# Attention over packed keys followed by a squared-relu MLP: batch 0 in two pieces with float keys, scores on 16 tiles from batch 3, small stages of both quads merged

## The chip, the cores and the metric

The kernel runs on one core of one Trainium2 chip. The metric is device time in microseconds (us), the median of the runs shown. The core has five engines that run their own instruction streams in order and wait for each other by semaphores: TensorE (PE, matmuls; its weight loads are listed as PEld), VectorE (DVE), ScalarE (ACT), GpSimd (POOL) and SyncE (SP). Transfers are issued from SP, ACT or POOL and run on 16 shared DMA engines.

## The reference

Eight batches of eight heads, 576 positions, head dimension 64, and 32 "pack" queries per head.

```python
def sm_attn(qq, kk, vv):
    s = scale * np.matmul(qq, kk.transpose(0, 1, 3, 2))
    s = s - np.max(s, axis=-1, keepdims=True)
    a = np.exp(s)
    a = a / (np.sum(a, axis=-1, keepdims=True) + 1e-09)
    return np.matmul(a, vv)
p_packed = sm_attn(p, k, v)             # 32 x 64 per head
out = sm_attn(q, p_packed, p_packed)    # 576 x 64 per head
...
x = np.ascontiguousarray(attn_out.transpose(0, 2, 1, 3)).reshape(B * S, H * D)   # 4608 x 512
h = x @ w_in                            # 512 x 2048
r = np.maximum(h, 0.0)
return ((r * r) @ w_out).astype(np.float32)                                       # 2048 x 512
```

All inputs are float32 with small random values; the output is float32.

## The kernel before

**One list sets the order of everything.** The string `ORDER` (L41 to L123) holds one word per step. `run` (L573) executes the words one after another in a manual schedule, so that each engine gets its instructions in the order of the words, and so does each DMA queue. There is no other scheduler. A letter after a colon names the engine of the step: `v` DVE, `a` ACT, `p` POOL.

**Tiles.** Four heads make a quad, so a batch has quads 0 and 1. A 128-partition tile of a quad holds four heads of 32 rows each.

The steps of a quad `bq` (batch b, quad q), in the order in which they depend on each other:

- `Lk`, `Lq`, `Lv`: loads of k, q, v, issued on POOL's queue, which turns float32 into bfloat16 in flight (`load1`, L229).
- `kT`, `qT`: DVE transposes of 32x32 blocks (L279, L285).
- `s1`: scores of the pack queries against the keys (`scores`, L295), 32x32 matmuls over 288 columns. One quad uses 4 of the array's 16 tiles of 32x32; where both quads are given in one step (`s12`, three characters) and the batch is in `PAIRED` (2 to 7), the second quad's heads are swapped by `group`, so that both quads use different tiles, 8 at a time. Such a step goes through four rounds: two halves of 288 columns by two halves of the 64-deep contraction.
- `m1` maximum (DVE, L316), `x1` exponential (ACT, L321), `rd` reciprocal of its sum (DVE, L328).
- `eT` six PE transposes of the exponentials (L339), `eo` their copy out of PSUM, `pv` 24 matmuls with v (L352), `pp` the normalised packed rows (L360, L362), `bd` a DVE transpose of them (L367), `pt` a PE transpose of them (L372) and `po` its copy out.
- `s2`: scores of the 576 positions against the 32 packed rows, the same form as `s1`.
- `t2` DVE transpose out of PSUM (L383), `m2` maximum over the 32 (L387), `sb` subtraction, called `d` (L391, DVE or POOL), `x2` exponential (L396, ACT), `su` sums and reciprocals (L401, L403), `a2` normalised weights, called `a` (L407, DVE or POOL), `aT` DVE transpose into `a2T` (L415).
- `w0`, `w1`: the packed rows times `w_in`, 8 matmuls each for 2 x 512 columns (L422), and `W0`, `W1`, their copies out of PSUM to `wp`.

The weights of the second attention are thus folded into the MLP: instead of forming x, the kernel multiplies `wp` (packed rows times w_in) with `a2T`.

The steps of the MLP:

- `h`: layer 1 for one block of 128 of the 2048 hidden columns (L438). From batch 1 on a step is `hb.half.block`, two matmuls of 288 positions. In batch 0 a step `h0.block` covers both halves in a two-bank PSUM tile, four matmuls.
- `r`: relu out of PSUM (ACT L444 or DVE L446), `q`: the square into `gT` (DVE L479).
- `o`: layer 2 (L490). `o<tile>.<j>` is two matmuls of 512 columns; 8 such steps make a tile of 128 positions, 36 tiles in all. Tiles 0 to 3 take the quarters of `w_out` in the order 0, 2, 1, 3.
- `c`: the copy of a finished tile out of PSUM, and its two stores, issued on SP (L510). The last tile is split over ACT and DVE.

`Wi`, `Wo` load `w_in` and `w_out` in quarters on POOL's queue; `P0`, `P1`, `Pr`, `Pt` bring and transpose the pack queries (`p_f` is loaded as float32 on SP at the start); `Z<n>` puts n matmuls of zeros on PE (L263), 95 in all, 32 of them before the first scores.

**PSUM.** `psa` has two tiles of two banks, for scores, transposes, `pv` and `w`. The other four banks change their use: three `spare` and one `idle` for batch 0's attention, then two two-bank tiles `pair` for batch 0's layer 1, then two `pso` and two `early` for tiles 0 to 3, and two `psh` for layer 1 later.

Of the kernel before, what the change touches and what calls it, by code (L numbers as in the profile page):

```python
# [31 lines left out]
PAIRED = range(2, 8)  # L32
# [9 lines left out]
Lk00 Lk01 Lq00 kT00 P0 Z32 s100 kT01 I m100 x100 Z5 s101 m101 x101 Lq01 P1 Z7 eT00 Lv00 eo00:a Lk10 Z10 pv00 rd00  # L42
qT00 rd01 qT01 pp00:v bd00 eT01 kT10 Lv01 Z3 s200 Wi00 Wi01 pt00 eo01:a Lk11 Z5 pv01 s110 pp01:a t200 pt01 Wi10 bd01
m200 sb00:p m110 s201 x110 t201 x200 m201 su00 Z10 eT10 po01:v eo10:a a200:v Z12 w001 sb01:p po00:a x201 su01 Wi11
aT00 w000 Lv11 a201:p kT11 W001:a Z11 s111 Lv10 W000:a aT01 h0.8 m111 h0.11 r0.8:a h0.9 r0.11:v h0.2 x111 r0.9:a
w101 q0.8 h0.3 r0.2:v W101:a Lq11 eT11 eo11:a rd11 h0.10 Lq10 q0.9 rd10 w100 r0.3:v W100:a h0.1 r0.10:v h0.0 q0.3
pv11 Wo0 r0.1:a q0.11 Pr r0.0:v h0.5 q0.2 pp11:a h0.6 pv10 r0.5:a qT11 r0.6:a pt11 bd11 q0.1 h0.14 pp10:a q0.10
r0.14:a h0.12 s211 h0.15 q0.0 r0.12:a h0.7 r0.15:a po11:v qT10 r0.7:a w011 Wo2 t211 Lk21 h0.13 q0.6 W011:a q0.5 h0.4
bd10 r0.4:a w111 s210 r0.13:v Wo1 o0.0 q0.7 m211 sb11:v o2.0 x211 W111:a t210 o2.1 Lk20 m210 o3.0 Wo3 o1.0 o0.1 o0.2
q0.15 o1.1 su11 o1.2 Pt pt10 po10:a q0.4 o2.2 o3.1 w010 Lv20 w110 o0.3 Lq21 o3.2 o3.3 o0.4 q0.13 o2.3 W010:a Lv21  # L50
o1.3 kT21 q0.12 W110:a kT20 a211:p o1.4 q0.14 sb10:p x210 su10 o1.5 o0.5 s12 o2.4 o2.5 a210:p m120 x120 o0.6 m121
o1.6 aT11 aT10 o0.7 c0:v o1.7 x121 o2.6 c1:a o2.7 h1.0.0 qT21 h1.0.6 eT20 eT21 rd21 r1.0.6:v rd20 r1.0.0:a o3.4
h1.0.4 Lq20 eo20:a h1.0.2 pv20 eo21:v pv21 r1.0.2:v r1.0.4:a h1.0.1 pp20:v h1.0.5 pt20 pp21:v c2:a r1.0.1:a r1.0.5:a
o3.5 po20:a bd21 h1.0.12 h1.0.3 w020 q1.0.2 o3.6 r1.0.12:a r1.0.3:a h1.0.7 h1.0.13 q1.0.0 Lk30 qT20 o3.7 W020:a bd20
o4.0 r1.0.13:a c3:a r1.0.7:v q1.0.1 h1.0.10 q1.0.6 h1.0.11 q1.0.3 s22 r1.0.10:a h1.0.8 r1.0.11:a r1.0.8:a h1.0.9
Lq30 o4.1 t220 h1.0.14 r1.0.9:a o4.2 t221 q1.0.4 r1.0.14:a h1.1.0 r1.1.0:a pt21 h1.0.15 m221 o4.3 po21:a h1.1.2
r1.0.15:a w021 w120 q1.0.5 h1.1.10 o5.0 sb21:v r1.1.2:a W021:a o4.4 h1.1.8 m220 x221 Lv31 r1.1.10:a sb20:v o5.1 Lk31
r1.1.8:a x220 o4.5 h1.1.3 r1.1.3:a h1.1.11 o4.6 r1.1.11:a kT30 W120:a h1.1.4 kT31 r1.1.4:a w121 q1.0.7 h1.1.1 o5.2
o4.7 r1.1.1:a h1.1.6 o5.3 su20 W121:a su21 Lq40 h1.1.5 r1.1.5:a r1.1.6:v c4:a o5.4 s13 a221:v h1.1.7 q1.1.0 r1.1.7:a
h1.1.14 q1.1.5 o5.5 r1.1.14:a h1.1.15 r1.1.15:a a220:v Lk40 o5.6 aT21 o5.7 q1.1.1 q1.1.2 h1.1.12 q1.1.3 Lk41 aT20  # L60
c5:a h1.1.13 Lq31 r1.1.12:a o6.0 o6.1 h1.1.9 r1.1.13:a r1.1.9:a o6.2 Lv41 m131 h2.0.2 q1.1.4 r2.0.2:a h2.0.3 o6.3
m130 h2.0.0 r2.0.3:a o6.4 h2.0.4 kT40 q1.1.7 r2.0.0:a x130 o7.0 h2.0.8 r2.0.4:a o6.5 Lv30 r2.0.8:a eT30 x131 h2.0.6
rd30 o7.1 eo30:v h2.0.7 o7.2 eT31 r2.0.6:a q1.1.6 o6.6 o6.7 qT30 r2.0.7:a rd31 qT31 q2.0.1 h2.0.1 h2.0.14 pv30
eo31:a r2.0.1:a pv31 o7.3 pp31:a c6:a r2.0.14:v h2.0.5 q2.0.0 o7.4 h2.0.10 pp30:a r2.0.5:v o7.5 bd30 r2.0.10:a
h2.0.12 pt30 r2.0.12:a o7.6 h2.0.9 h2.0.11 po30:a kT41 w030 bd31 w130 r2.0.11:a W030:a r2.0.9:v q2.0.3 h2.1.6 q2.0.2
r2.1.6:a h2.0.13 o7.7 r2.0.13:a o8.0 W130:v c7:a h2.0.15 h2.1.7 r2.0.15:a s23 q2.0.4 h2.1.0 r2.1.7:v q2.0.7 o8.1
r2.1.0:a h2.1.14 t230 o8.2 t231 h2.1.12 r2.1.14:a Lq41 q2.0.6 m231 o8.3 o8.4 Lv40 r2.1.12:a pt31 q2.0.5 h2.1.1 o8.5
o9.0 h2.1.15 r2.1.1:a h2.1.4 r2.1.4:a o8.6 r2.1.15:a o9.1 o8.7 m230 h2.1.10 po31:v sb31:v o9.2 h2.1.13 x231 o9.3
o9.4 r2.1.10:a sb30:v su31 r2.1.13:a h2.1.8 q2.1.3 c8:a w131 w031 q2.1.0 h2.1.11 o9.5 x230 r2.1.8:v r2.1.11:a a231:v
W031:a q2.1.6 h2.1.2 o9.6 r2.1.2:v h2.1.5 su30 o9.7 a230:v q2.1.7 h2.1.3 aT31 W131:a r2.1.5:a o10.0 o10.1 o10.2 s14  # L70
h2.1.9 aT30 c9:a r2.1.3:a o10.3 q2.1.1 h3.0.8 o10.4 o10.5 r2.1.9:a r3.0.8:a h3.0.2 h3.0.0 m140 q2.1.4 x140 m141
r3.0.2:a x141 q2.1.2 q2.1.5 o11.0 eT40 eo40:v h3.0.6 o11.1 r3.0.0:a rd41 o11.2 h3.0.3 eT41 r3.0.6:a h3.0.1 qT40 qT41
r3.0.3:a o10.6 Lk50 eo41:a r3.0.1:v h3.0.7 o10.7 rd40 q3.0.1 pv40 pv41 r3.0.7:a pp40:v q3.0.0 h3.0.4 h3.0.5 pt40
o11.3 r3.0.4:a h3.0.9 c10:v Lk51 o11.4 r3.0.5:v r3.0.9:a q3.0.4 o11.5 h3.0.10 o11.6 po40:a pp41:a h3.0.12 pt41 bd40
r3.0.10:a q3.0.3 h3.0.14 r3.0.14:v r3.0.12:a o11.7 h3.0.15 bd41 w140 po41:a q3.0.2 w040 r3.0.15:v h3.1.2 W040:a
o12.0 W140:a o12.1 r3.1.2:v h3.0.11 o12.2 o12.3 kT51 q3.0.7 r3.0.11:v h3.1.0 kT50 s24 h3.1.4 r3.1.0:v c11:a o12.4
t241 o12.5 r3.1.4:a o12.6 h3.1.5 o12.7 r3.1.5:a h3.0.13 q3.0.5 r3.0.13:a o13.0 h3.1.6 o13.1 m241 c12:a sb41:v h3.1.3
# [48 lines left out]
class Kernel:  # L126
# [138 lines left out]
    def bank32(self, b, name):  # L265

        if b == 0:
            return self.banks("spare").tile([P, 512], F32, name=name, tag="s")
# [359 lines left out]
```

## Time and profile before

| | |
|---|---|
| runs: median (lowest to highest) | 251.08 us (250.28 to 251.39), 3 runs |
| span of the profiled execution | 248.6 us |
| PE busy | 237.1 us, 2415 matmuls |
| DVE busy | 194.2 us, 411 instructions |
| ACT busy | 145.7 us, 316 |
| POOL busy | 45.8 us, 75 |
| layer 2 (L490), busy | 144.2 us |
| layer 1 (L438), busy | 91.9 us |
| read from HBM, written | 37.22 MB, 9.44 MB |

The span reaches from the first to the last instruction; the time of a run is longer by what lies around it. Matmuls are pipelined, so the busy time of one line overlaps that of the next: a mean duration in the groups (379 ns for L490) is a latency, and the distance from one matmul to the next is read from the chain of waits, where matmuls of one kind follow each other. The groups of the profile give line, engine, operation, output and inputs with their shapes, count, then busy time and mean duration in ns of one, then idle time of the engine before them and what ended it.

### The profile page before, as it was taken

Reading aid. Unit: us, or ns where it says so; the run is one execution under the profiler, and the core shown is the slowest. Engines: PE = TensorE matmul, PEld = TensorE weight load, DVE = VectorE, ACT = ScalarE, POOL = GpSimd, SP = SyncE. Lnnn points to the kernel's source line nnn. Section 1 sums busy time; section 2 is a strip of 40 time slices with the busy share of each in tenths; the row PEclk is TensorE's granted clock in tenths of the full one; section 3 lists DMA queues with packets and bytes.
Section 4 is the critical chain, followed back from the end, with each engine's and each line's share of the span. In section 5 each row is a group of like instructions: output and inputs, shape, how many; then the busy total and the mean of one; then the engine's idle time right before and its main releaser. Section 6 shows DMA issues by size and latency. Waiting matters only on the chain.

```text
span 248.6 us, 6041 instructions
## 1 busy us (share of the span) xinstructions
PE 237.1 (95%) x2415; PEld 132.2 (53%) x2447; DVE 194.2 (78%) x411; ACT 145.7 (59%) x316; POOL 45.8 (18%) x75
## 2 busy tenths in 40 slices
PE   8998899998999999999999999999999999999992
PEld 5655554465556554655456555655555555555540
DVE  1888899978988899979887998898897798644710
ACT  2346784476968748755764658676957555353100
POOL 8329634350401500033000230010000000000000
PEclk9999999999999999999999999999999999999997
DMA  6999999999791992269812794252121213211323
GB/s 112 203 207 205 206 197 209 197 142 259 161 171 64 157 211 45 46 93 187 185 42 45 135 130 122 64 90 56 42 45 42 45 42 82 49 42 44 70 63 82
DMA packets 23358, 28.52 MB, mean 115 GB/s; under 512 B 4257, under 2 KB 14753, under 8 KB 23329
## 3 DMA queue, kind: packets, MB, share of 16 engines
q0 software_dynamic: 16880, 18.55, 47.1%
q1 hardware_dynamic: 6288, 9.44, 15.0%
q8 instruction: 19, 0.31, 0.5%
q10 hardware_dynamic: 160, 0.13, 0.2%
q14 instruction: 11, 0.08, 0.1%
HBM read 37.22 MB, written 9.44 MB: 188 GB/s over the span
## 4 chain that ended last, share of the span: by engine, by line
PE 81%; DMA 10%; issue 2%; DVE 2%; POOL 2%; ACT 1%; SPq 0%; ACTq 0%; POOLq 0%
PE ps_o L490 48%; PE ps_h L438 24%; DMA v_b<-in_v_dram 4%; PE ps_wp L422 3%; PE ps_s L295 3%; DMA w_in_bf<-in_moe_w_in_dram 3%; DMA out_dram<-o_sb 3%; PE ps_e1T L339 1%; PE ps_pv L352 1%; POOL k_b L242 1%; DVE mx L387 1%; POOL d L391 0%; ACT r L444 0%; POOL q_b L242 0%; PE ps_ppT L372 0%
## 5 line engine op out<-in xcount | busy, mean ns | idle before, releaser
L490 PE MATMUL ps_o<-w_out_bf,gT 128*128 128x512 bf16 x544 | 144.2, 379 | 2.0 <-issue 0.5
L444 ACT ACTIVATE r<-ps_h 128x288 bf16<-128x288 f32 (+1 forms) x181 | 73.1, 426 | 55.9 <-PE ps_h L438 47.5
L438 PE MATMUL ps_h<-a2T,wp 128*128 128x288 bf16 x512 | 91.9, 286 | 1.4 <-ACT r L444 1.4
L490 PEld LDWEIGHTS <-gT 128*128 128x128 bf16 x576 | 54.9, 98 | 42.1 <-issue 3.3
L438 PEld LDWEIGHTS <-wp 128*128 128x128 bf16 x512 | 47.4, 98 | 44.4 <-issue 7.7
L479 DVE TENSOR_TENSOR gT<-r 128x576 bf16<-128x576 bf16 x128 | 54.7, 448 | 5.2 <-ACT r L444 4.9
L446 DVE TENSOR_SCALAR r<-ps_h 128x288 bf16<-128x288 f32 (+1 forms) x59 | 28.5, 484 | 20.0 <-PE ps_h L438 18.8
L332 ACT CAST wp<-ps_wp 128x1024 bf16<-128x1024 f32 x29 | 28.9, 1016 | 3.8 <-PE ps_wp L422 3.7
L332 ACT COPY o_sb<-ps_o 128x512 f32<-128x512 f32 x27 | 15.9, 588 | 10.8 <-PE ps_o L490 9.4
L321 ACT ACTIVATE e<-ps_s,nm 128x576 bf16<-128x576 f32 x16 | 11.8, 736 | 13.0 <-DVE nm L316 13.0
L233 POOL DMA_DIRECT2D v_b<-in_v_dram x16 | 11.1, 695 | 44.2 <-PE ps_pv L352 22.5
L279 DVE STREAM_TRANSPOSE kT<-k_b 128x576 uint32<-128x576 uint32 x16 | 15.0, 943 | 5.1 <-DMA k_b<-in_k_dram 5.1
L263 PE MATMUL ps_idle<-nought 128*128 128x288 bf16 x95 | 14.4, 304 | 1.1 <-DVE nought L178 1.1
L383 DVE STREAM_TRANSPOSE s<-ps_s 128x576 f32<-128x576 f32 x16 | 12.0, 767 | 2.4 <-PE ps_s L295 2.4
L401 DVE TENSOR_REDUCE sums<-e 128x18 f32<-128x576 f32 x16 | 11.9, 741 | 1.4 <-ACT e L396 1.3
L242 POOL DMA_DIRECT2D k_b<-in_k_dram x16 | 9.0, 562 | 21.4 <-DVE kT L279 12.5
L422 PE MATMUL ps_wp<-w_in_bf,ppT 64*32 64x512 bf16 x256 | 11.4, 382 | 0.8 <-DMA w_in_bf<-in_moe_w_in_dram 0.7
L316 DVE TENSOR_REDUCE nm<-ps_s 128x1 f32<-128x576 f32 x16 | 11.6, 739 | 0.6 <-PE ps_s L295 0.6
L285 DVE STREAM_TRANSPOSE qT<-q_b 128x576 uint32<-128x576 uint32 x16 | 12.0, 761 | 0.0
L387 DVE TENSOR_REDUCE mx<-s 128x18 f32<-128x576 f32 x16 | 11.9, 743 | 0.1
L396 ACT ACTIVATE e<-d 128x576 f32<-128x576 f32 x16 | 11.0, 685 | 1.6 <-DVE d L391 1.4
L263 PEld LDWEIGHTS <-nought 128*128 128x128 bf16 x95 | 9.2, 103 | 4.9 <-issue 1.2
(47 smaller groups left out, 153.0 us busy)
## 6 DMA issues: line engine op xcount, KB each, us to landing
out_dram<-o_sb SPq DMA_DIRECT2D x70, 128.0 KB, 2.8
k_b<-in_k_dram POOLq DMA_DIRECT2D x16, 288.0 KB, 8.1
v_b<-in_v_dram POOLq DMA_DIRECT2D x16, 288.0 KB, 7.4
q_b<-in_q_dram POOLq DMA_DIRECT2D x10, 288.0 KB, 7.2
w_in_bf<-in_moe_w_in_dram POOLq DMA_DIRECT2D x4, 512.0 KB, 12.5
w_out_bf<-in_moe_w_out_dram POOLq DMA_DIRECT2D x4, 512.0 KB, 13.8
q_b<-in_q_dram POOLq DMA_DIRECT2D x12, 144.0 KB, 3.9
p_b<-in_p_dram POOLq DMA_DIRECT2D x1, 192.0 KB, 11.5
```

The lines of the kernel that those rows point to most:

```text
L263: self.nc.tensor.matmul(ps[:, :HALF], lhsT=self.nought[:, :P], rhs=self.nought, start=True, stop=True)
L279: return self.nc.vector.transpose(t["kT"][:].rearrange("p (j l a) e -> p a j l e", j=J, a=3).bitcast(U32).rearrange("p a j l e -> p a j (l ...
L285: return self.nc.vector.transpose(t["qT"][:].rearrange("p s e -> p (s e)").bitcast(U32), t["q"][:].rearrange("p t d -> p (t d)").bitcast(U32))
L332: engine.copy(out, x)
L383: nc.vector.transpose(s2[:].rearrange("p (a t) i -> p a (t i)", a=2), t["ps_s2"][:, :, :HALF])
L387: self.nc.vector.tensor_reduce(out=t["mx"], in_=t["s2"], op=ALU.max, axis=AX.X)
L422: self.nc.tensor.matmul(ps[NP * h:NP * h + NP, c, :], lhsT=t["ppT"][D * c:D * c + D, NP * g:NP * g + NP], rhs=self.w_in_bf[D * c:D * c + D ...
L438: self.nc.tensor.matmul(ps, lhsT=t["wp"][:, fb // n, fb % n * P:(fb % n + 1) * P], rhs=t["a2T"][:, hf * HALF:(hf + 1) * HALF], start=(qd = ...
L444: engine.activation(r, ps, ACT.Relu)
L446: engine.tensor_scalar_max(r, ps, 0.0)
L479: (engine or self.nc.vector).tensor_tensor(out=out, in0=r, in1=r, op=ALU.mult)
L490: self.nc.tensor.matmul(self.o[tt], lhsT=self.gT[:, fb, a:a + P], rhs=self.w_out_bf[:, fb, :], start=(i == 0), stop=(i == self.NFB - 1))
```

## The change

**Batch 0 in pieces.** Its keys are no longer cast in flight on POOL's queue: they are loaded as float32 on SP's queue into a corner of `gT` that is not in use yet, and cast on DVE and ACT by new steps `ka`, `kb`. The float packs `p_f` are now loaded behind them on the same queue (step `pf`). The second attention of batch 0 and its layer 1 are cut at 320 of 576 positions (`PARTS`): steps `tA mA sA xA uA aA TA` and `tB ... TB` take the place of `t2 ... aT`, and the `h0` steps become 32 halves of 320 and 256 columns with their own relus and squares, six of the squares on POOL. The first half of `w` for batch 0 is cut in two, and so is the first half of `w_in` (six loads in place of four).

**Sixteen tiles.** For batches 3 to 7 (`WIDE`) the two halves of the 288 columns use different rows of tiles. For this the second half of k and q is loaded with its rows shifted by 32 partitions (more and smaller loads), the transposed packs get a shifted copy `pT1` (step `Pu`, two transfers on SP), and the packed rows a shifted copy (step `bs`, two transfers on SP per batch).

**Merged stages.** From batch 1 on (`PAIRED` is now 1 to 7) `s1`, `rd`, `pv`, `pp`, `bd`, `pt`, `po` and `s2` take both quads in one step; one PSUM tile, one copy and one DVE instruction serve both.

**Elsewhere.** The other four PSUM banks are now two pools of two, `x` for layer 2 and `y` for layer 1, from batch 0's layer 1 on. The stores are a step of their own, `d`, apart from the copy `c`. The scaling of the later packs moves from DVE to ACT (`Px`). The list is written anew: `d` (step `sb`) is on POOL 13 times of 14 and `a` 12 of 14 from batch 1 on (before 3 and 3 of 16); relus from batch 1 on are 147 on ACT and 77 on DVE (before 171 and 53); 14 of the output copies are on DVE (before 8); 44 idle matmuls are left, none ahead of the first scores. POOL issues 104 loads in place of 63 and 37 arithmetic operations in place of 6; SP issues 87 transfers in place of 73.

```diff
-PAIRED = range(2, 8)
+PAIRED = range(1, 8)
+WIDE = range(3, 8)
+PARTS = {False: ((0, HALF), (HALF, S)), True: ((0, 320), (320, S))}
...
-Lk00 Lk01 Lq00 kT00 P0 Z32 s100 kT01 I m100 x100 Z5 s101 m101 x101 Lq01 P1 Z7 eT00 Lv00 eo00:a Lk10 Z10 pv00 rd00
...
+Lk00 I Lk01 pf Lv01 Lq00 Lv00 Lq01 ka00:v kb00:a Wi01 kT00 Wi00 ka01:a P0 Wi11 kb01:a P1 s100 Wi10 kT01 m100 Z5 s101
+Wi20 x100 m101 x101 Wi21 Z6 eT00 qT00 eo00:a Z2 eT01 rd00 rd01 eo01:v Lk11 pv00 pp00:v pv01 pt00 bd00 pp01:a po00:v
...
-    STAGES = ((("spare", 3), ("idle", 1)), (("pair", 2),), (("pso", 2), ("early", 2)), (("psh", 2),))
+    STAGES = ((("spare", 3), ("idle", 1)), (("x", 2), ("y", 2)))
...
+        if word == "Pr":
+            self.nc.gpsimd.dma_start(self.p_b[:, x, :], self.packed(x.start, x.stop))
+        elif word == "Px":
+            self.nc.scalar.mul(self.p_b[:, x, :], self.p_b[:, x, :], SCALE)
+        elif word == "Pt":
+            self.p_turn(x.start, x.stop)
+        else:
+            self.nc.sync.dma_start(z[NP:], y[:P - NP])
+            self.nc.sync.dma_start(z[:NP], y[P - NP:])
...
-    def load_w_in(self, c2, c):
+    def load_w_in(self, n, c):
+        f0, f1 = ((0, 256), (256, 512), (512, 1024))[n]
...
+    def load_rows(self, x, s, n=0):
+        n *= NP
+        self.nc.gpsimd.dma_start(x[n:], s[:P - n])
+        if n:
+            self.nc.gpsimd.dma_start(x[:n], s[P - n:])
...
+        if (n, b) == ("k", 0):
+            f = self.gT[:, self.NFB - 2:, :].rearrange("p f s -> p (f s)").bitcast(F32)[:, qd * T * D:(qd + 1) * T * D]
+            t["f"] = f.rearrange("p (t d) -> p t d", d=D)
+            self.nc.sync.dma_start(t["f"], s)
+        elif b not in WIDE:
+            self.load_rows(x, s, g)
+        else:
+            for hf in range(2):
+                if n == "k":
+                    y = slice(hf * J // 2, (hf + 1) * J // 2)
+                    self.load_rows(*(z.rearrange("p (a j) d -> p a j d", j=J)[:, :, y, :] for z in (x[:], s)), hf)
+                else:
+                    y = slice(hf * T // 2, (hf + 1) * T // 2)
+                    self.load_rows(x[:, y, :], s[:, y, :], g + hf)
...
+    def st_cast(self, t, n, engine):
+        x = slice(n * T // 2, (n + 1) * T // 2)
+        self.copy(engine, t["k"][:, x, :], t["f"][:, x, :])
...
-    def scores(self, *quads):
-        for hf in range(2):
+    def scores(self, parts, *quads):
+        for w in ((0, 1),) if len(quads[0][1]) > 1 else ((0,), (1,)):
             for e in range(2):
                 for ps, x, y, tiles in quads:
-                    for r, c in tiles:
...
+                    for hf in w:
+                        s0, s1 = parts[hf]
+                        for r, c in tiles:
+                            r = (r + hf * (len(x) - 1)) % QH
...
+    def st_shift(self, b):
+        x, y = self.att[b, 0]["ppd2"], self.tp.tile([P, 2, 2 * NP], BF16, name="ppd1")
+        self.nc.sync.dma_start(y[NP:], x[:P - NP])
+        self.nc.sync.dma_start(y[:NP], x[P - NP:])
...
+    def st_pv(self, b, *qds):
+        ps = self.bank32(b, "ps_pv", len(qds))
+        for j in range(J):
+            for i, qd in enumerate(qds):
+                t = self.att[b, qd]
+                t["ps_pv"] = ps
+                for h in range(QH):
+                    g = NP * self.group(b, qd, h)
+                    self.nc.tensor.matmul(ps[g:g + NP, i, :D], lhsT=t["e1T"][:, j, g:g + NP],
+                                          rhs=t["v"][:, h, j, :], start=(j == 0), stop=(j == J - 1))
...
+    def st_ppT(self, b, *qds):
+        t = self.att[b, qds[0]]
+        t["ps_ppT"] = self.bank16(b, "ps_ppT")
+        for i, qd in enumerate(qds):
+            self.nc.tensor.transpose(t["ps_ppT"][:, i * P:(i + 1) * P], t["pp"][:, i].rearrange("p c d -> p (c d)"), self.ident)
...
-    def step_h(self, engine, b, *x):
-        if b == 0:
-            fb, = x
-            ps = self.ph[b, fb] = self.banks("pair").tile([P, 2, 512], F32, name="ps_h2")
-            for hf in range(2):
-                self.layer1(ps[:, hf, :HALF], b, fb, hf)
...
+    def step_h(self, engine, b, hf, fb):
+        s0, s1 = PARTS[b == 0][hf]
+        ps = self.ph[b, hf, fb] = self.bank("y" if b or fb % 2 else "x", "ps_h")
+        self.layer1(ps[:, :s1 - s0], b, fb, s0, s1)
```

## The prediction

> **What bounds the kernel now.** I read the busy shares in slices first, then the chain of waits, then the same chain in order of time, then the groups and the timeline. The slices:
>
> ```profile
> PE   8998899998999999999999999999999999999992
> DVE  1888899978988899979887998898897798644710
> DMA  6999999999791992269812794252121213211323
> ```
>
> A slice is 6.2 us. PE is full from slice 14 to the end; DMA is full for the first eight. The chain by engine, and pieces of it in order of time (start, duration):
>
> ```profile
> PE 81%; DMA 10%; issue 2%; DVE 2%; POOL 2%; ACT 1%; SPq 0%; ACTq 0%; POOLq 0%
> ...
> 5.27 9.11 DMA v_b<-in_v_dram
> ...
> 18.31 1.10 POOL d L391
> 19.41 7.36 DMA w_in_bf<-in_moe_w_in_dram
> 27.22 0.60 PE ps_h L438 x4
> ...
> 28.15 0.49 PE ps_h L438 x4
> ...
> 42.26 0.56 PE ps_wp L422 x16
> ...
> 46.98 0.63 PE ps_s L295 x29
> ...
> 233.02 4.32 PE ps_o L490 x20
> ```
>
> The reader is to see two regimes: until about 27 us the chain is loads and small stages, after that PE lines, back to back. They also give prices in a full stream: an `o` matmul 4.32/20 = 0.215 us, an `h` matmul 0.49/4 = 0.1225, one step of scores 0.63, `w` 0.56 for two quads.
>
> In the timeline the first `h` starts at 23.14 (F), the first `h` of batch 1 at 51.04, the last `o` ends at 243.84, and 4.8 us of copy and store follow. I split the span as F + PE work behind F + idle behind F + tail. Work of the order of before at those prices (transposes of `e` 0.34 a quad, `pv` 0.27 a quad and 0.49 for two, `ppT` 0.22, near its 221 ns row): 24.7 us between F and 51.04 (h0 7.8, 56 `o` matmuls 12.0, small stages 4.9), and 190.1 us after it. Idle is therefore 27.9 - 24.7 = 3.2 and 192.8 - 190.1 = 2.7 us. Behind 23 us there are only 5.9 us that any reordering could win; the rest must come from F or from less PE work.
>
> **The change part by part.**
>
> *PE work.* Scores of batches 3 to 7 now run as two rounds over 16 tiles instead of four rounds over 8. One round is 288 columns, 0.12 us at the `h` price, so 0.63 is four rounds and 0.15 of filling; two rounds come to 0.39. No row of before shows 16 tiles. From below the bound is the issue rate: 48 `pv` matmuls take 0.49, so 32 take 0.33. From above it is 0.63, no gain. I take 0.39, nearest to the rounds: 10 steps x 0.24 = 2.4 us. Batch 1 in pairs saves two score steps, 1.3; `ppT` for both quads at once 7 x 0.2 = 1.4; `pv` 7 x 0.05 = 0.35. In before, two scores and one transpose of batch 1 lay ahead of F (1.6 us); now they come behind it. Work behind F: 214.8 - 2.4 - 1.3 - 1.4 - 0.35 + 1.6 = 211.0 us.
>
> *The start.* The keys of batch 0 move from POOL's queue to SP's as float32, the float packs `p_f` move behind them, and casts are added (ACT three, DVE one). In before `p_f` took 2.2 us from issue to landing; keys issued on POOL at 1.25 landed at 5.6 and the next at 7.1, so 0.295 MB of bf16 (0.59 MB read) every 1.5 us, 205 GB/s written. At that read rate SP's 1.3 MB take 3.2 us after a first byte near 1.8; POOL's queue starts about 2 us later and shares at the end, so `p_f` lands between 5.5 and 8.2. I take 6.4, near the unshared end, and the first scores at 7.1, as before (7.05). From there by rows, second quad, which is last: `kT` ends 8.95 (behind two casts of 0.68), scores 0.95, maximum 0.95, exponential 0.95, transposes 0.8, copy 0.7, `pv` 0.6, `pp` 0.65, `bd` 0.4, `qT` 0.75, scores 0.9 = 16.6 us. Then piece A of 320 columns, prices of 576 cut by size: transpose 0.8 and maximum 0.8 behind the other quad's pieces, `d` on POOL 0.85, `e` 0.55, sums 0.8, `a` 0.5, the other pieces and `a2T` 0.6, hand-over 0.25: 21.8 us, against F 23.14. The first half of `w_in` needs 2.9 MB written ahead of it, 14.1 us at 205 GB/s, about 17 to 18: hidden. Loads of k, v, q of batch 1 and w_out add 4.8 MB and end near 42 us; the last quarter of w_out is asked for near 45, so they are hidden by 3 us. Bounds for F: 19.5 and 24.5.
>
> The 32 idle matmuls at the start go, and 51 in all. Idle matmuls in half-microsecond windows:
>
> ```profile
> 2.00:2.50 0.50, 0.50 (x4) 0.30 (x3) 1.00 0.97 218
> ...
> 4.50:5.00 0.50, 0.50 (x6) 0.40 (x5) 1.00 1.05 189
> ```
>
> The column in brackets counts matmuls touching the window: they came slower at first, though the granted clock reads 1.00. A cold first pass costs up to one more duration of scores, transposes and `pv`, about 1 us on the chain; I leave it to the upper bound. The Trainium skill, "TensorE: Matmul & The Clock Gate", Part 1, says that the array runs at half clock until about 3.4 us of activity. By that rule F would be near 22.8; the trace agrees with the slow first matmuls, without showing the cause.
>
> *Idle up to h1.* The relus and squares of batch 0 now come in 32 halves. Rows:
>
> ```profile
> L444 ACT ACTIVATE r<-ps_h 128x288 bf16<-128x288 f32 x171 | 66.8, 412 | 53.5 <-PE ps_h L438 46.5 <-DVE r L446 2.1 <-DVE rden L328 1.2
> L446 DVE TENSOR_SCALAR r<-ps_h 128x288 bf16<-128x288 f32 x53 | 24.0, 453 | 18.1 <-PE ps_h L438 17.0 <-issue 0.4
> L479 DVE TENSOR_TENSOR gT<-r 128x576 bf16<-128x576 bf16 x128 | 54.7, 448 | 5.2 <-ACT r L444 4.9
> ```
>
> ACT has 23 (12 of 320 columns at 0.44, 11 of 256 at 0.385) and one `wp` copy of 1.0: 10.5 us. DVE has 9 (4.0), some eight squares (3.5), a `wp` copy 1.2, one `kT` 0.95, the rest of piece B 1.3: 11.0 us. PE's part is 8.4, so 2.6 us idle. Then batch 1: from second scores to h1 the order has 8.1 us of PE work; the chain is two transposes 1.5, two maxima 1.5, `d` 0.75, `e` 0.7, sums 1.0, `a` on POOL 1.16, `a2T` 0.45, six hand-overs of 0.2, and batch 2's `kT` 0.95 between: 9.2, so 1.1 to 1.8 idle. I take 4.4 in all (2.6 if the chain is hidden, 8 if POOL's queue delays it) against 3.2.
>
> *Idle behind h1.* `d` and `a` move from DVE to POOL (6 whole ones to 25, with the pieces and squares 37 operations), about 19 x 0.78 = 15 us off DVE; 24 relus, 6 output copies and six `wp` copies go onto it, about 22 us. DVE stays near 200 us. POOL issues 104 loads instead of 63, each about 0.55: some 57 us, besides 35 us of arithmetic; it stays below half. The shift copies are two transfers on SP behind the stores: issue 0.64 and landing 2.0 to 2.8, against PE work from `bd` to scores of 4.0 to 11.1 us, but 2.7 in batch 7: I take 0.4. 2.7 + 0.4 = 3.1 (1.5 to 10, the top from the first rival).
>
> *Tail.* The stores of tile 34 now stand 1 us ahead of those of tile 35 on SP: +0.2 (0 to 0.6). Moving the store into a step of its own issues the same transfers in the same queue, at nothing else.
>
> **Sum.** 21.8 + 211.0 + 4.4 + 3.1 = 240.3, against 243.84; with the tail -3.3 us, a span of 245.3. The page gives the span 248.6 and the runs a median of 251.08; I take the 2.5 us outside the span as unchanged: **247.8 us**.
>
> **Rivals.**
>
> *POOL holds up DVE (slower).* Two operations on POOL and the squares beside them:
>
> ```profile
> 41.47 1.15 POOL L407 TENSOR_TENSOR a<-e,rs 128x576 bf16<-128x576 f32 x1 [1.02 <-DVE rs L403]
> 42.59 1.26 POOL L391 TENSOR_TENSOR d<-s,mx 128x576 f32<-128x576 f32 x1
> ...
> 42.76 1.77 DVE L479 TENSOR_TENSOR gT<-r 128x576 bf16<-128x576 bf16 x2
> ```
>
> One square ended only after POOL, 1.40 us (the longest of the line) instead of 0.45; reductions and transposes beside the other POOL operations kept their times. From second scores to the next `h` the new order has 9.8 to 12.4 us of PE work (13.4 to 15.4 before), the chain with both `d` on POOL takes 9.1 and what DVE puts between. If two squares a batch are held by 0.95 each, the margin of 0.7 to 3.3 is gone and PE waits about 1.2 us in each of 6 or 7 batches: 247.8 + 7.5 = 255.3. It decides from about 1.3 us a batch. Against it: it is one square of 128, and the trace has too few meetings for a rule. The Trainium skill, "GPSIMD Engine Reference", Key points, says POOL shares its SBUF interfaces with VectorE, in contention with instructions of two SBUF inputs; a square has two, and by that rule all 25 would count.
>
> *The start wins nothing.* Keys queue before `p_f`, PE is cold: F 24.0, so 250.0.
>
> *Sixteen tiles run no faster than eight* (the change not doing what it says): +2.4, 250.2.
>
> *Everything comes off.* F 19.5, idle 2.6 and 1.5: 247.8 - 2.3 - 1.8 - 1.6 = 242.1.
>
> **How the numbers follow.** Forecast 0.45, POOL 0.21, start 0.15, tiles 0.06, everything 0.13. 0.5% is 1.25 us, about what a measurement here tells from no change: faster below 249.8, slower above 252.3. The forecast, the good case and a third of the two middle ones give 0.65 faster; the rest of them 0.14 same; POOL 0.21 slower. The range 243.0 to 253.0 leaves out most of POOL's case and the edge of the good one; the likeliest's own is 245.5 to 250.
>
> **What would show it.** Steps of scores at 0.39 in the chain from batch 3 on; the first `h` near 21.8 us, h1 near 52; the median square still 0.45 with few above 1 us; PE waits on `a2T` at each new batch under 0.5 us. It is wrong if the squares' mean rises above 0.6, if scores stay at 0.6, or if F lies behind 23.

## The result and the profile after

The changed kernel takes 261.19 us (median; 260.77 to 263.69, 4 runs), the kernel before 251.24 us on the same chip: a ratio of 1.040 (95% interval 1.033 to 1.047). It is slower; the forecast was 247.8. Its profiled execution has a span of 259.1 us, 10.5 more than before. All times here are medians of runs in the fast state; one run of `e4` and two of `e11` were in a slower one and are left out.

The busy shares in slices (6.5 us each) of the changed kernel:

```profile
PE   0797789999989997989998998989999998999992
DVE  2589995899899876997799977998798888976721
POOL 8348883393498860382049420541035003300000
DMA  7999999999948997049224975347034401230233
```

PE is no longer full behind the start: a 7 or 8 stands about once in every batch. DMA is full up to the eleventh slice, and mostly not behind it. The chain that ended last, by engine, then pieces of it in order of time (start, duration):

```profile
PE 55%; DVE 29%; DMA 8%; issue 3%; ACT 2%; POOL 0%; SPq 0%; DVEq 0%; POOLq 0%
...
1.66 6.00 DMA p_f<-in_p_dram
8.25 1.15 PE ps_s L337 x14
...
24.48 1.90 DVE gT L559
...
34.87 2.81 DVE gT L559 x3
...
95.40 5.77 DMA ppd<-ppd
...
153.94 5.77 DMA ppd<-ppd
...
168.50 1.29 DVE gT L559
...
211.86 3.45 DMA ppd<-ppd
```

Before, PE had 81% of this chain. Now three things stand in it that the forecast priced at little or nothing: the load of the packs, single squares (`gT`) of 1 to 2 us, and the shift copies (`ppd<-ppd`). What PE waited for (total us, times, longest):

```profile
PE ps_s L337 <- DMA ppd<-ppd: 3.3, 3, 1.5
PE ps_o L570 <- DVE gT L559: 2.4, 4, 0.7
PE ps_h L532 <- DVE a2T L505: 2.1, 2, 1.8
PE ps_e1T L378 <- ACT e L365: 1.8, 2, 1.1
PE ps_h L532 <- DVE r L539: 1.6, 2, 0.8
```

Behind the first scores this view has 12.2 us of waits; in the kernel before it has 3.4, the largest of them 1.4 us for relus. The groups:

```profile
L559 DVE TENSOR_TENSOR gT<-r 128x576 bf16<-128x576 bf16 (+2 forms) x122 | 63.7, 536 | 5.3 <-ACT r L537 3.3
...
L476 POOL TENSOR_TENSOR d<-s,mx 128x576 f32<-128x576 f32 (+2 forms) x17 | 18.3, 1087 | 75.1 <-DVE mx L470 75.1
...
L496 POOL TENSOR_TENSOR a<-e,rs 128x576 bf16<-128x576 f32 (+1 forms) x14 | 15.4, 1108 | 12.9 <-DVE rs L490 11.2
```

The squares' mean rose from 448 to 536 ns, and that mean hides two kinds: 101 squares of about 0.45 us, and 21 that overlapped a computation of POOL (for 256, 288 and 320 columns by two 0.78, 0.90 and 1.43 us on average, 1.98 at most). Of these 21, five began 0.2 to 0.3 us ahead of POOL's operation and kept their time (0.36 to 0.47 us). The other 16 were held (one of them although it began 0.44 us ahead): each ended 0.28 to 0.36 us after an operation of POOL. The timeline shows two of the held ones:

```profile
24.19 0.63 POOL L496 TENSOR_TENSOR a<-e,rs 128x256 bf16<-128x256 f32 x1
24.40 1.98 DVE L559 TENSOR_TENSOR gT<-r 128x640 bf16<-128x640 bf16 x1
24.77 1.25 POOL L559 TENSOR_TENSOR gT<-r 128x640 bf16<-128x640 bf16 x1
26.66 0.81 PE L532 MATMUL ps_h<-a2T,wp 128*128 128x256 bf16 x6 [1.78 <-DVE a2T L505]
...
168.31 1.16 POOL L496 TENSOR_TENSOR a<-e,rs 128x576 bf16<-128x576 f32 x1 [0.77 <-ACT e1T L371]
168.42 1.72 DVE L559 TENSOR_TENSOR gT<-r 128x576 bf16<-128x576 bf16 x2
169.84 1.04 PE L570 MATMUL ps_o<-w_out_bf,gT 128*128 128x512 bf16 x4 [0.69 <-DVE gT L559]
```

The square of 24.40 ends only after both operations of POOL, `a2T` stands behind it in DVE's queue, and PE waits 1.78 us. At 168.42 the first of two squares ends 0.3 us after POOL's `a`, and PE waits 0.69 us. DVE's reductions, its transposes, and its relus and copies out of PSUM kept their times beside POOL. The one `d` that is left on DVE, which also has two inputs in SBUF, began beside a `d` of POOL and took 1.22 us, where DVE's took 0.75 in the kernel before.

In the prediction's terms, as differences from before (F: start of the first `h`; PE work by the distances between matmul starts in the trace, one `o` 0.2155, one `h` 0.1225, small stages 26.3 before and 24.1 after; idle is what is left of the time from F to the end of the last `o`):

| us against before | forecast | changed kernel | last experiment (`e18`) |
|---|---|---|---|
| F (before 23.1) | -1.3 | -0.7 (22.4) | -0.6 |
| PE work behind F (213.2) | -3.8 | -2.3 | -2.3 |
| idle behind F (7.5) | +1.6 | +13.4 | +6.5 |
| tail (4.8) | +0.2 | +0.1 | -0.3 |
| span (248.6) | -3.3 | +10.5 | +3.3 |

Nearly all of the loss is idle of PE: from F to the first `h` of batch 1 the kernel takes 32.5 us (before 27.9), and behind that each batch up to batch 6 has one or two gaps of 0.6 to 1.8 us.

### The profile page after: what moved, and what is told of

Same layout as the page of the kernel before. It is cut to its first block, busy times and chain, and to the rows that moved or that the text cites. A ratio compares the mean times of both kernels' runs of the same rounds, so it can differ in the third digit from the quotient of the medians.

```text
span 259.1 us, 6108 instructions
## 1 busy us (share of the span) xinstructions
PE 233.2 (90%) x2412; PEld 124.9 (48%) x2412; DVE 210.0 (81%) x422; ACT 128.7 (50%) x284; POOL 105.1 (41%) x147
## 4 chain that ended last, share of the span: by engine, by line
PE 55%; DVE 29%; DMA 8%; issue 3%; ACT 2%; POOL 0%; SPq 0%; DVEq 0%; POOLq 0%
PE ps_o L570 31%; PE ps_h L532 16%; DVE gT L559 8%; DMA ppd<-ppd 6%; DVE sums L488 3%; DVE r L539 3%; DVE mx L470 3%; PE ps_s L337 3%; DVE s L457 2%; DMA p_f<-in_p_dram 2%; DVE wp L373 2%; PE ps_e1T L378 2%; DVE qT L324 1%; DVE rs L490 1%; PE ps_pv L399 1%
## 5 line engine op out<-in xcount | busy, mean ns | idle before, releaser
L537 ACT ACTIVATE r<-ps_h 128x288 bf16<-128x288 f32 (+2 forms) x170 | 65.0, 412 | 74.2 <-PE ps_h L532 65.8
L532 PE MATMUL ps_h<-a2T,wp 128*128 128x288 bf16 (+2 forms) x512 | 90.9, 287 | 4.3 <-DVE a2T L505 2.1
L559 DVE TENSOR_TENSOR gT<-r 128x576 bf16<-128x576 bf16 (+2 forms) x122 | 63.7, 536 | 5.3 <-ACT r L537 3.3
L539 DVE TENSOR_SCALAR r<-ps_h 128x288 bf16<-128x288 f32 (+2 forms) x86 | 38.2, 450 | 13.3 <-PE ps_h L532 12.8
L476 POOL TENSOR_TENSOR d<-s,mx 128x576 f32<-128x576 f32 (+2 forms) x17 | 18.3, 1087 | 75.1 <-DVE mx L470 75.1
L371 ACT CAST wp<-ps_wp 128x1024 bf16<-128x1024 f32 (+1 forms) x24 | 22.8, 963 | 7.5 <-PE ps_wp L516 7.4
L496 POOL TENSOR_TENSOR a<-e,rs 128x576 bf16<-128x576 f32 (+1 forms) x14 | 15.4, 1108 | 12.9 <-DVE rs L490 11.2
L250 POOL DMA_DIRECT2D q_b<-in_q_dram x26 | 14.2, 551 | 2.1 <-DVE qT L324 1.9
L373 DVE COPY o_sb<-ps_o 128x512 f32<-128x512 f32 x14 | 9.6, 684 | 6.5 <-PE ps_o L570 6.4
L482 ACT ACTIVATE e<-d 128x576 f32<-128x576 f32 (+2 forms) x18 | 11.1, 637 | 4.2 <-POOL d L476 4.2
```

The source lines that it names most:

```text
L250: self.nc.gpsimd.dma_start(x[n:], s[:P - n])
L371: engine.copy(out, x)
L373: engine.tensor_copy(out, x)
L476: engine.tensor_tensor(out=d2[:, x], in0=t["s2"][:, x], in1=t["mx"][:, x].unsqueeze(2).to_broadcast([P, n, NP]), op=ALU.subtract)
L496: engine.tensor_tensor(out=a2[:, y].rearrange("p t i e -> p t e i"), in0=t["e2"][:, x].rearrange("p (t e) i -> p t e i", e=2), in1=t["rs"] ...
L532: self.nc.tensor.matmul(ps, lhsT=t["wp"][:, fb // n, fb % n * P:(fb % n + 1) * P], rhs=t["a2T"][:, s0:s1], start=(qd == 0), stop=(qd == se ...
```

## The experiments

The theory is that DVE's squares wait for POOL wherever `d`, `a` or POOL's own squares run, and that the new order has too little PE work beside the chain to hide it. The rivals: DVE has too much work; the shift copies are late; the start is late; the order itself.

### POOL's arithmetic moved to DVE: `e1`, `e9`, `e10`

```diff
-sb11:p ... sb10:v ... a211:p ... a210:p
+sb11:v ... sb10:v ... a211:v ... a210:v
```

`e1` does this for all 25 `d` and `a` of batches 1 to 7.

> The 25 whole d and a operations of batches 1 to 7 go back from POOL to DVE. First theory (POOL holds the squares, and that is most of the lost time): no square of batches 1 to 7 stays above 0.6 us, their mean is 0.45; DVE gives back about 10 us of holding for 25 x 0.78 = 19.5 us of new work, and still the time falls by 3 to 7 us, to 254 to 258. Rival (DVE simply has too much to do, the holding costs nothing by itself): DVE busy rises from 210 to about 220 us and the time rises to 262 to 268. Rival (late shift copies are the cause): within 1.3 us of 261.

270.99 us, ratio 1.078 (1.071 to 1.084): 10 us worse. Its group of squares and its waits:

```profile
L559 DVE TENSOR_TENSOR gT<-r 128x576 bf16<-128x576 bf16 (+2 forms) x122 | 56.4, 476 | 5.3 <-ACT r L537 3.4
```

```profile
PE ps_o L570 <- DVE gT L559: 6.6, 5, 2.5
PE ps_h L532 <- DVE a2T L505: 3.3, 5, 1.6
```

From batch 1 on the squares take 0.447 us on average and 0.46 at most, so the holding is gone, yet PE waits longer for the same tiles. DVE runs one queue in order: `d` and `a` now stand ahead of the squares and of the other quad's stages. Undoing the move does not measure the holding; it swaps it for a longer chain. `e9` takes work off DVE at the same time (26 relus, 8 `W` and 8 `c` steps to ACT):

> The changed kernel with both earlier edits at once: the 25 d and a of batches 1 to 7 on DVE, and the 42 relus and copies on ACT. DVE has about 192 us of work, as before the change, no square of batches 1 to 7 is held by POOL, and d and a take 0.75 us, not 1.2 to 1.4 one behind the other. Fourth theory (from second scores to the next h the chain through two d and two a on POOL is 10 to 11 us long by itself, as long as PE's filler; adding work to DVE lengthens it and taking relus off DVE cannot shorten it): the chain falls by 1 to 1.5 us a batch, time 252 to 256. Rival (ACT's relus and copies now stand in the chain, or the order itself is too tight): 259 or more.

272.27 us, 1.080 (1.073 to 1.086). `e10` moves only the second quad's `d` and `a` (12 operations), with the 26 relus on ACT:

> Of the two d and two a of a batch the second ones go to DVE (12 operations, +9 us of DVE), the first ones stay on POOL, and 26 relus go to ACT (-11.8 us of DVE). Fourth theory: the two quads' operations run beside each other, the chain is 1 to 1.5 us shorter in each batch, 254 to 258. If DVE's load alone counted: it is about 4 us lower with the squares that are no longer held, 257 to 260. If neither: 261 to 264, as with the relus alone.

265.93 us, 1.055 (1.049 to 1.061). All three are slower than the changed kernel, which fits that POOL beside DVE shortens the chain even while it holds squares up.

### Less work for DVE: `e5`, `e6`

```diff
-r1.0.5:v ... c7:v ... W031:v
+r1.0.5:a ... c7:a ... W031:a
```

`e5` moves 26 relus of batches 1 to 6 to ACT, `e6` also 8 `W` and 8 `c`.

> The changed kernel with 26 of the 66 DVE relus of batches 1 to 6 on ACT. DVE has 11.8 us less to do (26 x 0.452), ACT 10.8 more. Third theory (DVE is the bound from the first h to the first h of batch 7, so every us of its work is a us of time; moving d and a to DVE gave 9.1 us of work and 9.8 us of time): the time falls by 8 to 12 us, to 249 to 253. Rival (single waits behind the attention's chain, whatever DVE's load): 258 to 261.

> As the run before, and 8 copies of wp (1.22 us each) and 8 of output tiles (0.68) go from DVE to ACT as well: DVE has 27 us less than in the changed kernel, ACT 24 more (153 us). Third theory: DVE is no longer the bound, PE is: first h 22.4 + work 211.4 + idle 5 to 8 + tail 5 + 2 outside the span = 246 to 249. Rival (waits of the chain): 255 or more. If ACT becomes the bound, 251 to 255.

263.06 us (1.046, 1.039 to 1.053) and 265.36 us (1.054, 1.049 to 1.060): no gain, a loss for `e6`. So less work on DVE alone does not bring the time back; whether work that became late on ACT took the place of it, these runs do not tell apart.

### Eight tiles again, and the shift without DMA: `e2`, `e3`, `e7`

`e2` empties `WIDE`, which also takes away the shift copies:

```diff
-WIDE = range(3, 8)
+WIDE = range(8, 8)
```

> WIDE is emptied: all scores on 8 tiles, no shift copies, loads of k and q in batches 3 to 7 whole again. PE work grows by 10 x 0.23 = 2.3 us. First theory (POOL's holding): the idle time stays, 262.5 to 264.5. Second theory (shift copies that land late, and the small loads that make the queues slow): the waits of 0.8 to 1.5 us for second scores in batches 3, 5 and 7 and what follows from them go, 4 to 6 us, so 257 to 260 in spite of the added PE work.

259.35 us, 1.032 (1.026 to 1.037). Ten steps of scores cost 0.22 us more each, and still it is not slower: what the 16 tiles win is lost again on what they need, the copies and the smaller loads. `e3` keeps the tiles and makes the shifted rows by four DVE transposes of 32 partitions:

```diff
-self.nc.sync.dma_start(y[NP:], x[:P - NP])
-self.nc.sync.dma_start(y[:NP], x[P - NP:])
+for i in range(QH):
+    j = (i + 1) % QH
+    self.nc.vector.transpose(y[NP * j:NP * j + NP].bitcast(U32), pp[NP * i:NP * i + NP, :, 0, :].bitcast(U32))
```

> The sixteen tiles stay, but the shifted copy of the packed rows is made by four small DVE transposes per batch (about 0.1 to 0.2 us each) and not by two transfers on SP. Second theory (late shift copies): scores no longer wait, 2.5 to 5 us come off, 256 to 258.7. First theory (POOL's holding): only the chain's few waits shift, 260 to 261.5; the squares stay as slow as they are (mean of those beside POOL 0.9).

259.68 us, 1.033 (1.028 to 1.038). The 3.3 us of waits are gone, and 1.5 us of the time: other waits took their place. Both ratios overlap that of the changed kernel, so neither gain is sure alone. `e7` is `e6` with this shift:

> As the run before, with the shifted packed rows made by four small DVE transposes a batch in place of two transfers. Second theory on top of the third: with DVE relieved, the late shift copies are all that is left behind the first h of batch 1, and without them 1.5 to 4 us come off: 243.5 to 247. If DVE was all there was, the same as the run before within 1 us.

261.1 us, 1.036 (1.031 to 1.042): 4.3 us less than `e6`, with intervals apart, and still no better than the changed kernel.

### The kernel before with POOL's `d` and `a`: `e4`

In the list of before, 24 steps `sb` and `a2` of batches 2 to 7 go from `v` to `p`.

> The kernel before with its 24 d and a operations of batches 2 to 7 moved from DVE to POOL, nothing else. First theory (POOL's holding): squares beside POOL rise from 0.45 to about 0.9, some up to 2 us, the chain from second scores to the next h grows by 2 to 4 us a batch, and the time goes from 251 to 256 to 261. Rival (holding is harmless, DVE is relieved by 19 us): 249 to 251.5.

261.0 us (3 runs), 1.031 (1.020 to 1.042). Here 20 more squares overlapped POOL (mean 0.80 us), and 11 of them took 0.53 to 1.41 us; yet from batch 3 on the first `h` of the batches are as far apart as before (28.0, 28.4, 26.3, 27.1 us against 28.0, 28.4, 26.3, 26.8). Nearly all of the loss lies in batches 1 and 2, and comes by another way, which POOL's timeline shows:

```profile
63.88 1.18 POOL L391 TENSOR_TENSOR d<-s,mx 128x576 f32<-128x576 f32 x1
...
74.02 2.49 POOL L407 TENSOR_TENSOR a<-e,rs 128x576 bf16<-128x576 f32 x2 [7.93 <-DVE rs L403]
...
78.59 1.41 POOL L233 DMA_DIRECT2D v_b<-in_v_dram  x2
```

`a` waits 7.93 us in POOL's queue, and the load of v behind it goes out at 78.59 instead of 67.07. In batch 1 it is a load of keys behind `d`, which goes out at 64.99 instead of 51.38. The chain shows its landing and the `kT` for which it was awaited, and a square stands behind that `kT` in DVE's queue; PE waits for it:

```profile
64.99 5.76 DMA k_b<-in_k_dram
...
70.77 0.94 DVE kT L279
```

```profile
PE ps_o L490 <- DVE gT L479: 4.3, 1, 4.3
```

That held squares cost nothing here from batch 3 on fits with the room that this order has: before, 13.4 to 15.4 us of PE work lie between the second scores and the next `h`, in the new order 9.8 to 12.4.

### The packs first: `e8`

```diff
-Lk00 I Lk01 pf Lv01 Lq00
+pf Z20 Lk00 I Lk01 Lv01 Lq00
```

> The changed kernel with the float packs loaded ahead of batch 0's keys on SP, and 20 idle matmuls on PE ahead of the first scores. Start theory (packs queued behind keys, PE cold): the first scores start at 6.2 to 7.0 us, not 8.25, and take 0.7 us, not 1.15; the first h comes at 20.3 to 21.4, not 22.4, and the time falls by 1 to 2 us, to 259 to 260.2. Rival (DVE or w_in sets the first h): first h at 22 or later, time unchanged.

259.71 us, 1.033 (1.026 to 1.039), an interval that overlaps the changed kernel's. PE at the start of this execution:

```profile
1.08 4.41 PE L298 MATMUL ps_idle<-nought 128*128 128x288 bf16 x20 [1.08 <-DVE nought L182]
7.25 0.69 PE L337 MATMUL ps_s<-kT,pT 32*32 32x288 bf16 x16 [1.77 <-DVE pT L220]
```

The first scores came 1.0 us earlier and took 0.69 us in place of 1.15; the first `h` came at 20.5. The last two experiments show that this is not to be relied on.

### Shorter operations on POOL: `e11`, `e12`

`e11` cuts POOL's `d` and `a` into pieces of at most 192 columns and its squares in two.

> Every POOL operation is cut in pieces (d and a in three of 192 columns, in batch 0 two, a square in two), nothing else: the same work on each engine, but a square that waits for POOL waits for a third of it. First theory (the holding of squares is what costs): held squares fall from a mean of 0.90 to 0.6 or less, DVE's busy time falls by 5 us or more, and the time falls by 2 to 5 us, 256 to 259. Rival (POOL's own latency in the chain): three pieces take 0.1 to 0.3 us longer than one, the time stays or rises, 260.5 to 264.

262.6 us (2 runs), 1.042 (1.036 to 1.049): the interval overlaps that of the changed kernel, so no change is shown either way. Squares, and waits:

```profile
L570 DVE TENSOR_TENSOR gT<-r 128x576 bf16<-128x576 bf16 (+2 forms) x122 | 59.5, 502 | 5.2 <-ACT r L547 3.3
```

```profile
PE ps_h L542 <- DVE a2T L515: 5.5, 5, 2.8
...
PE ps_o L581 <- DVE gT L570: 0.3, 1, 0.3
```

The holding shrinks on the whole, and PE hardly waits for `gT` (2.4 before the cut), but POOL's busy time grows from 105.1 to 117.7 us, and the wait for `a2T` grows from 2.1 to 5.5. Half of that is one square, which the cut did not help: it starts at 25.40, takes 2.94 us and ends 0.35 us after the last of five pieces that follow each other on POOL without a gap; `a2T` stands behind it, and PE waits 2.8 us. `e12` is `e9` with the shift by DVE, the packs first and batch 0's POOL squares on DVE:

> All helpful edits together: d and a of batches 1 to 7 on DVE, 42 relus and copies on ACT, the six POOL squares of batch 0 on DVE, shift by DVE transposes, float packs first and 20 idle matmuls ahead of the first scores. Fourth theory: the gains add up, 9 to 12 us below the changed kernel, 249 to 252. Rival (each wait that goes is replaced by the next in an order with too little slack): 255 to 259.

265.71 us, 1.055 (1.051 to 1.060), though no square took more than 0.79 us.

### The same instructions with one input: `e13`, `e14`

This is the direct test. The instruction stays in its place, takes as long alone, and reads one operand; it is another operation, so the squares are left out of the result:

```diff
-(engine or self.nc.vector).tensor_tensor(out=out, in0=r, in1=r, op=ALU.mult)
+if engine is self.nc.gpsimd:
+    engine.tensor_tensor(out=out, in0=r, in1=r, op=ALU.mult)
+else:
+    self.nc.vector.transpose(out.bitcast(U32), r.bitcast(U32))
```

> The changed kernel in which DVE's squares are left out: in the place of each stands a 32x32 block transpose of the same tile into the same place (one input in SBUF where the square has two; transposes of this size take 0.45 us, and none was held by POOL in any trace). Order, engines, POOL's operations, transfers and the six squares on POOL are as they were. First theory (POOL's holding of two-input squares is what costs): no such instruction above 0.6 us, and 7 to 11 us come off, 250 to 254. Rival (length of the chain, late shift copies, order without slack): 258 to 261.5.

256.39 us, 1.022 (1.016 to 1.028): 4.8 us less, with intervals apart. Group and waits:

```profile
L562 DVE STREAM_TRANSPOSE gT<-r 128x288 uint32<-128x288 uint32 (+2 forms) x122 | 54.9, 461 | 6.6 <-ACT r L537 3.7
```

```profile
PE ps_s L337 <- DMA ppd<-ppd: 4.0, 3, 2.5
PE ps_h L532 <- ACT r L537: 2.8, 4, 2.1
PE ps_h L532 <- DVE a2T L505: 0.7, 2, 0.3
...
PE ps_o L573 <- DVE gT L562: 0.3, 1, 0.3
```

None of the 122 took more than 0.51 us though POOL does what it did; the 24 that overlapped POOL took 0.45 on average. The waits for `gT` and `a2T` fall from 4.5 to 1.0, and F to `h1` takes 29.1 us instead of 32.5. `e14` adds the shift by DVE:

> As the run before, and the shifted packed rows are made by four small DVE transposes a batch in place of the two transfers. If the holding and the late copies are two causes that add up: 3 to 5 us less than the run before, 246 to 250, near what was predicted for the change. If the copies only showed because of the holding: within 1 us of the run before.

253.55 us, 1.008 (1.006 to 1.011): another 2.8 us less, nearly twice what the same edit gave in `e3`. That would fit held squares that had hidden part of the late copies; since the 1.5 us of `e3` are unsure themselves, it is not shown.

### A complete version in a new order: `e15`, `e16`

`e15` computes everything: no squares on POOL, 39 on ACT, 24 whole `d` and `a` on POOL, some 30 relus exchanged each way between ACT and DVE, the shift by DVE, the packs and 20 idle matmuls first, and the words of the list moved so that fewer squares meet POOL. `e16` has the same engines for the steps in the changed kernel's order.

> A complete version of the changed kernel: 36 of its squares on ACT and none on POOL, some 30 relus exchanged between ACT and DVE in each direction, d and a still on POOL 23 times, the shift made by four small DVE transposes a batch, float packs first, 20 idle matmuls ahead of the first scores, and the words in a new order in which squares and POOL's operations seldom meet. If holding, late copies and the start were the causes: no square on DVE above 0.8 us, first h near 20.5 us, and a time of 246 to 251, at or below the kernel before. Rival (the merged, sixteen-tile form has too short a distance between second scores and the next h whatever the order): 254 to 260.

> The order of the changed kernel, with the same changes of engines, shift, packs and idle matmuls as the run before, but no word moved apart from the packs. If the meetings of squares and POOL are the cause, moving squares to ACT is most of the gain: 252 to 256. If it is the order: 257 to 262.

`e15`: 252.26 us (10 runs), 1.004 (1.001 to 1.007). `e16`: 255.76 us, 1.017 (1.014 to 1.021). The chain of `e15` is PE's again:

```profile
PE 78%; ACT 7%; DVE 7%; issue 3%; DMA 2%; POOL 1%; SPq 0%; ACTq 0%
```

Ten squares still meet POOL (mean 0.58 us). The other engines, the shift and the start give 5.4 us together, the order 3.5 more. That comes to the kernel before, not below it; no version here beat it.

### All three causes: `e17`, `e18`

`e17` is the changed kernel with the packs first (as `e8`) and the shift by DVE (as `e3`); `e18` is `e17` with the one-input instructions of `e13`.

> The changed kernel with the packs' load and 20 idle matmuls first and the shift by DVE transposes, squares as they are. If the two costs stand beside each other, 261.2 - 1.5 - 1.5 = 258.2 us. If the held squares eat what an earlier start brings (POOL's d and a meet the next square on DVE instead), 259.5 or more. If the start and the shift copies were the main cause and only hid behind each other, below 256.

> The same two edits, and DVE's squares replaced by 32x32 block transposes of the same length with one input (the squares are left out). Theory that the three named causes make up nearly all of the miss: 248.5 to 250.5 us, close to the forecast of 247.8, first h near 20.5 to 21 and PE waits behind it of 3 to 5 us. Theory that a fourth cause of 3 us or more is left (the tighter order itself, late stores that hold output buffers): 251.5 to 253 us, 253.55 less the 1.5 to 2 us of the start.

`e17`: 259.33 us, 1.029 (1.023 to 1.034). `e18`: 253.60 us (12 runs), 1.007 (1.004 to 1.010). Their difference, 5.7 us on one chip, is the price of the holding with the other two out of the way. (Of the 5.9 us between the two profiled executions 1.2 lie ahead of F, where no square runs, so 4.7 is the safer figure.) Its place can be read from the same two traces, whose PE work is the same: from the second scores to the next `h`, batches 2 to 7 take 70.7 us together in `e17` and 65.3 in `e18`, and from F to the first `h` of batch 1 it is 32.0 and 29.2. But `e18` is no faster than `e14`: the start gave nothing here. PE at the start of `e17`:

```profile
1.07 4.98 PE L298 MATMUL ps_idle<-nought 128*128 128x288 bf16 x20 [1.07 <-DVE nought L182]
8.59 0.69 PE L337 MATMUL ps_s<-kT,pT 32*32 32x288 bf16 x16 [2.53 <-DVE pT L220]
...
10.69 1.15 PE L337 MATMUL ps_s<-kT,pT 32*32 32x288 bf16 x16 [0.69 <-DVE kT L318]
```

The first scores come later and run at full speed, the second at the slow one; between 10 and 12 us the windows give a granted clock of 0.50. In `e18` already the first took 1.15. Twenty idle matmuls ahead do not keep the array fast in every execution, and F was 20.5, 23.7 and 22.5 in `e8`, `e17` and `e18`. What `e18` still waits for:

```profile
PE ps_h L534 <- ACT r L539: 2.7, 3, 2.2
...
PE ps_o L575 <- DVE gT L564: 0.9, 2, 0.6
PE ps_h L534 <- DVE a2T L507: 0.8, 2, 0.4
```

The 2.2 us are an output store: it took 5.97 us in the chain (median of all stores 2.5), a copy to the same buffer waited for it on ACT, and relus stood behind.

## Why the prediction was wrong, step by step

**The step that failed is "idle behind h1 3.1", and with it "idle up to h1 4.4".** By the prices of the table the changed kernel's 20.9 us of idle are 14.3 behind the first `h` of batch 1 (h1) and 6.6 ahead of it. Both terms took squares beside POOL at nothing, and the rival that priced them had 0.21, because "it is one square of 128, and the trace has too few meetings for a rule". That was the wrong way to read one square. Before, POOL had 6 operations, and the only square that ran beside one of them was held to its end. The change brings POOL to 37 operations, so what counted was held squares per meeting, one of one, not per square. Of 21 that overlapped POOL, 16 were held; above the 0.41 to 0.48 us of the same shapes alone they cost DVE 10.7 us. `e13` prices them at 4.8 us of time and `e17` against `e18` at 4.7 to 5.7; the rival had 7.5, so it came nearest, but it was still 6 us short of the time.

Its place was half right. In the stretches that the rival named, from the second scores to the next `h`, the held squares cost 5.4 us in batches 2 to 7. With them gone, these stretches have 3.0 us of idle in `e18` by the prices of the table, against 5.0 in the kernel before, though they hold some 3 us less PE work each: without the holding the thinner cover did no harm. The other 2.8 us lie ahead of h1, where the prediction had looked at the sums of work of each engine alone; there the idle falls to 3.3 us, below the forecast 4.4. The sum of these two is more than the time that came off, because other waits, the late store above all, took part of their place. The Trainium skill, "SBUF — State Buffer", section "Who interferes with whom", says that a DVE instruction with two SBUF inputs contends with a GpSimd instruction that reads SBUF, and calls the shared port pair an exclusive lock; the squares, the one `d` on DVE, the one-input transposes and the reductions here agree with it.

**Shift copies, 0.4.** They were priced by a landing of 2.0 to 2.8 us; they landed in 1.8 to 5.8 (median 4.6), 5.77 twice in the chain. Taking them away gave 1.5 us in `e3`, unsure, and 2.8 in `e14`. The cover named for them, PE work from `bd` to the scores, was right; the size of the landing was that of the stores (medians of 2.0 to 2.8), not of copies like these.

**F, 21.8.** 22.4: off by 0.6. `p_f` landed at 7.66 instead of 6.4, and the first scores ran at the slow rate, 1.15 us instead of 0.69, as the prediction had left to its upper bound. `e8` points to 1.5 us that could be won; `e18` does not confirm it.

**PE work behind F, 211.0.** 210.9, right for a wrong reason. One `ppT` was priced at 0.22, a latency; from one start to the next it is 0.056, alone or merged. So before had 213.2, not 214.8, and the merged `ppT` saved nothing in place of 1.4. The 16 tiles were right: 0.41 us a step, predicted 0.39, against 0.63.

**The tail**, 0.2, was 0.1. The 2.5 us outside the span set the span of one execution beside the median of three; in the changed kernel's profiled execution 1.8 us lie outside (260.88 against 259.1).

**What is settled and what is open.** Of the 13.4 us between forecast and result, 7.6 go when the three causes are taken away (261.2 to 253.6). Of the 5.8 left, about 0.7 is F and 1.5 the saving of PE work that was not there. The rest is idle behind F: 14.0 us in `e18` by the table, where the forecast had 7.5 on a before of 5.9. Of these 14.0, 10.7 lie behind h1, and 7.7 of them outside the stretches from second scores to `h`, where the kernel before has none by the same prices. The late store, 2.2 us, is one piece of it, and some 3 us lie in gaps too small for the view of waits. Why the new order has this idle stays open. `e15` against `e16`, which differ in the order of the words alone, shows that order is worth 3.5 us of time.

**The signs named beforehand** did not fire though the kernel was slower: the squares' mean rose to 0.536 (limit 0.6), scores fell, F stayed below 23. Of the signs for being right, h1 came at 54.9 instead of near 52, and 10 squares took above 1 us. A limit on a mean of 122 cannot show 16 long ones; "few above 1 us" was the better sign.

## What to carry to other kernels

When work is moved to an engine, count its meetings with the instructions it has been seen to hold up, and price each by the one meeting in the trace: a rare event under the old order is no evidence of a rare event under the new. The same delay cost nothing where an order had 3 us more of PE work beside the chain (`e4` from batch 3 on), so price the margin together with the delay. A stage's cost on a pipelined engine is the distance between starts, not the mean duration of its row.

## What was not expected of the hardware

- A DVE square can wait through several operations of POOL back to back, not only the one that had begun (24.40: 1.98 us, ending with POOL's second; in `e11` 2.94 us, ending with the fifth). It is not always so: at 72.22 a square ended 0.31 us after the first of two `d` that followed each other without a gap. What decides it, no run here shows.
- Whether the array runs at full or half rate at the start changes from one run to the next: the first scores took 0.69 or 1.15 us behind the same 20 idle matmuls. The record of the granted clock can read 1.00 while they take 1.15 (`e18`); in `e17` it reads 0.50. The Trainium skill, "TensorE: Matmul & The Clock Gate", Part 1, says that the window of activity runs freely and does not start with the kernel; that fits, and no run here tests it.
- Copies from SBUF to SBUF of 8 to 24 KB took up to 5.8 us in the changed kernel, and stores up to 6.1 us in `e18` and 7.9 in the kernel before (medians 2.5 and 2.6).
- A step into scores, `pv` or `w` starts 0.093 us later than the same matmul stream would (`o` to `s` 0.309, `o` to `o` 0.216), 36 to 39 times in either kernel: some 3.5 us that neither sum had.
